# A transformer block on one core: two more tiles transposed by DMA, and work moved between slots and engines

## The chip, the core and the metric

The kernel runs on one core of a Trainium2 chip. A core has a matrix engine (TensorE, PE in the profile, with its weight loads as PEld), a vector engine (DVE), a scalar engine (ACT), GpSimd (POOL), and a sync engine (SP) that issues most DMAs here. Each engine works through its own queue in order and waits on semaphores where it needs what another has made. The metric is the device time of one execution in microseconds (us); 2% and less matter here, so times are compared as medians of several runs.

## What is computed

One pre-norm transformer block on x of 2048 positions by 512 channels, in float32: attention over a dilated local window, then a dense MLP with a squared ReLU.

```python
def _A_ref(x, wqkv, wo):           # H = 32 heads of 16, W = 8, dil = 2
    qkv = ...(x @ wqkv)...
    idx = pos[:, None] - (jnp.arange(W) * dil)[None, :]
    logits = jnp.einsum("bhsd,bhswd->bhsw", q, kg) * scale
    attn = _softmax(jnp.where(mask, logits, -1e9))
    o = jnp.einsum("bhsw,bhswd->bhsd", attn, vg)
    return o @ wo
def _B_ref(x, w1, b1, w2, b2):     # F = 1792
    r = relu(x @ w1 + b1)
    return (r * r) @ w2 + b2
h = x + _A_ref(_layernorm(x), wqkv, wo)
out = h + _B_ref(_layernorm(h), w1, b1, w2, b2)
```

## The kernel before

**Tiles and halves.** The positions are cut into 16 tiles of 128, four tiles to a group. Every operand of a matmul is split into a high half, a rounded copy made by ACT (`hi`, L151), and a low half, the difference, made by DVE or POOL (`lo`, L154, recorded as L155). A product is three sets of matmuls: high by high, low by high, high by low (`mm3`, L218; L228 in the profile). One product of a 128 x 512 tile is 12 matmuls.

**Phases.** First, 16 short products of the q, k, v projection; then a first phase (`first_phase`, L1007) that goes on with this projection for tiles 4 to 15, two tiles at a time, each as six half-products; then the MLP in four stages, u = 0 to 3, one for each group of four tiles. Stages 0 to 2 (L1087) have 17 steps p: at each step TensorE makes one block of w1's product (`mlp1`) and, three steps later, that block's product with w2 (`mlp2`, L895). Attention on DVE and POOL runs beside all this, as far as stage 2.

**Attention.** For each item (two rows of positions, two or four groups of heads), DVE multiplies q and k (L339), reduces (L373), and multiplies weights and v (L350); POOL adds up these products in three steps (`add_up`, L407), the last of which writes the result `o`. `stream` is a generator of these steps.

**The slots.** The order on all engines is written out by the program. `end_slot(pe)` (L122) closes a slot: it adds the planned TensorE time `pe`, runs what is registered for this slot with `at` (the list `due`), then `pump`s the attention generator until its planned DVE time has caught up with TensorE's, then runs what is registered with `midway` (the list `amid`; `pump` itself runs it once DVE's plan is within `HALF` = 2.6 us of TensorE's), then what is registered with `after` (the list `late`). So in DVE's queue a chore in `due` stands ahead of the slot's attention work, and a chore in `late` behind it. In the first phase a slot is half a product; `k` counts these halves from 0 to 23 over tiles 12 to 15, and `chores(k)` runs right after the slot before it is closed.

**From attention to the MLP, tile by tile.** At `OT[t]` the result of tile t is transposed on TensorE (`o_T`, L592): four 128 x 128 transposes into one PSUM bank, then `hi_T` and `lo_T`, both registered in `due`. At `WO[t]` follows its product with wo (`wo_product`, L683), and from it, slots later, the residual `h` and its norm's sums (`h_add`, L659, with `norm_stats`, L159), the normalised residual `hn` (`h_norm`), `add_b2` and a store of h (`spill`). The norm's three small factors are made on POOL by `finish` (L168). The normalised residual must then be transposed, too, to be the moving operand of stage u: by TensorE (`h_T`, L697), or, for tiles in `HV`, by DMA: ACT splits it into two 16-bit planes (`h_split`, L616), SP issues a transposing DMA (`turn_dma`, L618), ACT joins the planes (`turn_join`, L623), and `h_parts` (L648) makes the halves. In the first phase `HK[t]` gives the slots of the split and of the join, `HT[t]` that of `h_parts` or of `h_T`. Groups 1 to 3 are treated the same way inside stages 0 to 2, at the steps `OP`, `WP`, `HP`; all their attention results are transposed by DMA (`OV`).

**Banks of PSUM.** All eight are in use. Transposes of x and o in the first phase take turns in two, tr0 and tr1, one for each call (`Turn`, L139). A bank may be written again when the last reader of what it held is done. For x (`x_T`, L468) these are `hi_T`, registered in `due`, and `lo_T`, registered in `late`:

```python
def x_T(t):
    tr = transposes(xt.pop(t))
    xT[t] = row("xh", (P, KB, P), F32R), row("xl", (P, KB, P), F32R)
    at(0, hi_T, tr, [xT[t][0]])
    after(0, lo_T, tr, [xT[t][0]], [xT[t][1]])
```

Tiles 14 and 15 of x are transposed at k = 7 and 8 (`XT`). In `chores` this comes first, and then, in a loop over t, `o_T`, the split and join, `wo_product` and `h_parts` of tile t.

**Weights.** In the first phase `weight_job` (L570) loads a piece of wo or w1 and, five slots later, makes its halves. In stage 0 `split_w2` (L1069) makes the halves of w2's block f at step p = f: the high one on ACT, the low one on POOL in `late`.

Of the kernel before, what the change touches and what calls it, by code (L numbers as in the profile page):

```python
# [31 lines left out]
HALF = 2.6  # L32
AS = (8, 9, 12, 13)
OV = tuple(range(4, 16))
HV = (0,1,4,5,8,9,12,13)
SLOW = 1.01, 1.08, 1.05
DELAY = 3
WJ = 2
XT = (9, 11), (7, 8)
OT = 4, 5, 10, 12  # L40
WO = 7, 9, 13, 15
HT = 20, 20, 21, 23
HK = (12, 18), (14, 19)
W2 = (18,)
LH = 3, 4, 10, 11
OP = 6, 7, 12, 13
WP = 9, 10, 13, 14
HP = 15, 15, 16, 16
UP = 14, 14, 15, 15
HL = (14, 0), (14, 1), (15, 0), (15, 1)  # L50
# [8 lines left out]
def block_kernel(ctx, tc, x, wqkv, wo, w1, b1, w2, b2, out):  # L59
    nc = tc.nc  # L60
# [39 lines left out]
    w2_h, w2_l = {}, {}  # L100

    def row(name, shape=(P, D), dt=F32):
        return work.tile(list(shape), dt, name=name, tag="row", bufs=ROWS)
# [9 lines left out]
    def at(delta, fn, *a):  # L113
        due.setdefault(now["slot"] + delta, []).append((fn, a))

    def after(delta, fn, *a):
        late.setdefault(now["slot"] + delta, []).append((fn, a))

    def midway(delta, fn, *a):
        amid.setdefault(now["slot"] + delta, []).append((fn, a))  # L120
# [15 lines left out]
    def dve(t):  # L136
        now["dve"] += t
# [13 lines left out]
    def hi(dst, src):  # L151
        nc.scalar.copy(dst, src)  # L152
# [6 lines left out]
    def norm_stats(key, src):  # L159
        st = small.tile([P, 6], F32, name="st")  # L160
        mv = small.tile([P, 2], F32, name="mv", bufs=4)
        rs = small.tile([P, 2], F32, name="rs", bufs=4)
        nc.vector.bn_stats(st, src)
        nc.vector.bn_aggr(mv, st)
        dve(0.93)
        stats[key] = mv, rs

        def finish():  # L168
            nc.gpsimd.tensor_scalar(out=rs[:, 1:2], in0=mv[:, 1:2], scalar1=EPS, scalar2=None,
                                    op0=ALU.add)  # L170
            nc.gpsimd.tensor_tensor(out=rs[:, 0:1], in0=rs[:, 1:2], in1=mhalf, op=ALU.pow)  # L171
            nc.gpsimd.tensor_scalar(out=rs[:, 1:2], in0=mv[:, 0:1], scalar1=rs[:, 0:1],
                                    scalar2=-1.0, op0=ALU.mult, op1=ALU.mult)
        after(0, finish)

    def act_stats(key, src):

# [262 lines left out]
    def x_stats(t):  # L440
        if t < XS:
            norm_stats(t, xt[t])
        else:
            act_stats(t, xt[t])
# [125 lines left out]
    def weight_job():  # L570
        h, l, src, k, c0, cn = jobs.pop(0)
        raw = row("raw")
        nc.sync.dma_start(raw[:, :cn], src[k * P:(k + 1) * P, c0:c0 + cn])

        def split():
            hi(h[:, k, c0:c0 + cn], raw[:, :cn])
            after(0, lo, nc.gpsimd, l[:, k, c0:c0 + cn], raw[:, :cn], h[:, k, c0:c0 + cn])
        at(5, split)


    hs, hn = {}, {}
# [10 lines left out]
    def o_T(t):  # L592
        s, j = divmod(t, RI)
        pump(until=s)
        tr = transposes(o_t[s][:, j, :])
        if t % R == RI:

            ohl = att.tile([P, 2, KB, P], F32R, name="ohl", tag="o", bufs=3)
            oT[t] = ohl[:, 0], ohl[:, 1]
        else:  # L600
            oT[t] = row("oh", (P, KB, P), F32R), row("ol", (P, KB, P), F32R)
        at(0, hi_T, tr, [oT[t][0]])
        at(0, lo_T, tr, [oT[t][0]], [oT[t][1]])
# [55 lines left out]
    def h_add(t, ps):  # L659
        h = hs[t]  # L660
        nc.vector.tensor_tensor(out=h, in0=ps, in1=h, op=ALU.add)
        dve(0.7)
        if t in AS:
            after(0, act_stats, t, h)
        else:
            norm_stats(t, h)
# [16 lines left out]
    def wo_product(t, slots):  # L683
        ps = turn["mm"].tile("wo")
        oh, ol = oT.pop(t)
        mm3(ps, lambda k: oh[:, k, :], lambda k: ol[:, k, :],
            lambda k: wo_h[:, k, :], lambda k: wo_l[:, k, :], lows_last=t in OV)
        for n, (fn, a) in zip(slots, ((h_add, (t, ps)), (h_norm, (t,)), (add_b2, (t,)),
                                      (spill, (t,)))):
            (after if fn in (h_norm, spill) else at)(n + (fn is add_b2), fn, *a)  # L690
# [6 lines left out]
    def h_T(t):  # L697
        if t // R == R - 1:
            return last_h_T(t)
        tr = transposes(hn.pop(t), "mm")  # L700
        i = t % R
        hs_, ls_ = [a[:, :, i] for a in hh], [a[:, :, i] for a in hl]
        if len(turn["mm"].tags) > 2:
            at(0, hi_T, tr, hs_)
        else:
            due.setdefault(now["slot"], []).insert(0, (hi_T, (tr, hs_)))
        at(0, lo_T, tr, hs_, ls_)
# [299 lines left out]
    def first_phase(t0):  # L1007
        def chores(m):
# [11 lines left out]
            if jobs and m % 3 == 0:  # L1020
                at(0, weight_job)
# [3 lines left out]
            for t in range(R):  # L1025
                if k == OT[t]:
                    at(0, load_h, t)
                    o_T(t)
                if t in HV and k == HK[t][0]:
                    at(0, h_split, t)  # L1030
                    after(0, turn_dma, ("h", t))
                if t in HV and k == HK[t][1]:
                    at(0, turn_join, ("h", t))
                if k == WO[t]:
                    wo_product(t, (1, 3, 4, 6))
                    now["pe"] += 2.73
                if k == HT[t]:
                    (at(0, h_parts, t) if t in HV else h_T(t))
            if k in W2:
# [29 lines left out]
    def split_w2(f):  # L1069
        raw = raws.pop(f)  # L1070
        hi(w2_h[f], raw)
        if f < 12:
            place[f] = free.pop(0)
            w2_l[f] = big_l[:, place[f]]
            at(1, stash, f)
        after(0, lo, nc.gpsimd, w2_l[f], raw, w2_h[f])

    def stash(f):
        nc.sync.dma_start(w2l_d[f], w2_l[f].bitcast(F32))
# [7 lines left out]
    for u in range(R - 1):  # L1087
# [11 lines left out]
        for i in js:  # L1099
            t = R * (u + 1) + i  # L1100
            if not end:
                a = i // 2 if u == 2 else 0
                o0 = OP[i] - a - (2 if i >= RI and t in OV else 0)
                if t in OV:
                    turned = [(o0, at, 0, o_split, t), (o0, at if i >= RI else after, i // RI, turn_dma, ("o", t)),
                              (o0 + 2, at, 0, o_join, t)]
                else:
                    turned = [(o0, o_T, t)]
                if t in HV:
                    h0 = 11 + i  # L1110
                    turned += [(h0, midway, 0, h_split, t), (h0, after, 0, turn_dma, ("h", t)),
                               (h0 + 2, at, 0, turn_join, ("h", t))]
                for p, *what in ((LH[i] - a, at, 0, load_h, t), *turned,
                                 (WP[i] - a, wo_product, t, (0, 1, 2 + 3 * a, 3 + 3 * a))):
                    todo.setdefault(p, []).append(what)
                p, h = (HP[i], i % 2) if u < 2 else HL[i]
                if t in HV:
                    todo.setdefault(p, []).append((at, 0, h_parts, t))
# [14 lines left out]
        for p in range(FB + LAG):  # L1133
            more = 0.0
            if p == FB:
                run(due)
                dve(HOLD)
            if u < 2 and p == FB - 2:
                dve(HOLD)
            for fn, *a in sorted(todo.get(p, []), key=lambda x: x[0] is wo_product):  # L1140
                fn(*a)
                more += 2.73 if fn is wo_product else 0.0
            if p < FB:
                mlp1(u, fs[p])
                more += 2.73
                if first:
                    at(0, split_w2, p)
                    if p + 1 < FB:
                        load_w2(p + 1)
            q = p - LAG  # L1150
            if q >= 0:
                f = fs[q]
                mlp2(u, f, acc, js, q == 0, q == FB - 1,
                     (lambda: half(p)) if p in halves else None)
                more += 2.74
                if f < 12 and (need or first and p < FB - LAG):
                    free.append(place.pop(f))
                    if need:
                        at(1, fetch, need.pop(0))
            end_slot(more)  # L1160
# [85 lines left out]
```

## Time and profile before

| | |
|---|---|
| median of 3 runs | 510.37 us (509.52 to 511.27) |
| the profiled execution | 510.24 us |
| its span, first to last instruction | 508.5 us |
| granted TensorE clock | 1.000 |
| DMA | 102.61 MB, mean 202 GB/s |

The span leaves out 1.74 us at both ends of the execution. A matmul is pipelined: it lasts about 390 ns in the records, but the next one of 512 columns starts 227 ns after it, so waiting is read from the starts. A row of a timeline has the start and the length in us, the engine, the line, the operation, what is written from what, the count, and in brackets the idle time ahead of it with what ended it.

### The profile page before, as it was taken

Reading aid. Unit: us, or ns where it says so; the run is one execution under the profiler, and the core shown is the slowest. Engines: PE = TensorE matmul, PEld = TensorE weight load, DVE = VectorE, ACT = ScalarE, POOL = GpSimd, SP = SyncE. Lnnn points to the kernel's source line nnn. Section 1 sums busy time; section 2 is a strip of 40 time slices with the busy share of each in tenths; the row PEclk is TensorE's granted clock in tenths of the full one; section 3 lists DMA queues with packets and bytes.
Section 4 is the critical chain, followed back from the end, with each engine's and each line's share of the span. In section 5 each row is a group of like instructions: output and inputs, shape, how many; then the busy total and the mean of one; then the engine's idle time right before and its main releaser. Section 6 shows DMA issues by size and latency. Waiting matters only on the chain.

```text
span 508.5 us, 7542 instructions
## 1 busy us (share of the span) xinstructions
PE 498.6 (98%) x2422; PEld 420.5 (83%) x2422; DVE 375.2 (74%) x507; ACT 305.3 (60%) x558; POOL 361.4 (71%) x439
## 2 busy tenths in 40 slices
PE   8999999999999999999899999999999999999997
PEld 7998778888888887787688888888888888998986
DVE  6479899999999778986898989988951137732233
ACT  4635687577447747478454548756457847566541
POOL 5714789895776999989959777977896364685610
PEclk9999999999999999999999999999999999999999
DMA  8678889899698799789576756997572272444212
GB/s 271 189 212 204 245 290 302 245 307 303 201 228 253 253 273 278 215 216 291 166 248 207 216 147 165 257 252 244 161 173 63 80 212 83 169 123 144 64 43 83
DMA packets 109359, 102.61 MB, mean 202 GB/s; under 512 B 29448, under 2 KB 77832, under 8 KB 109320
## 3 DMA queue, kind: packets, MB, share of 16 engines
q1 hardware_dynamic: 108376, 101.61, 68.0%
q10 hardware_dynamic: 944, 0.52, 0.3%
q8 instruction: 19, 0.31, 0.2%
q14 instruction: 20, 0.16, 0.1%
HBM read 72.65 MB, written 24.25 MB: 191 GB/s over the span
## 4 chain that ended last, share of the span: by engine, by line
PE 66%; POOL 14%; DVE 2%; issue 2%; DMA 2%; ACT 1%; SPq 0%; POOLq 0%; ACTq 0%; DVEq 0%
PE mm L228 30%; PE acc L895 22%; PE wo L228 6%; PE mm L818 6%; POOL pr L407 5%; POOL rl L155 3%; POOL big_l L155 3%; PE tr L201 2%; POOL h L674 1%; DVE pr L350 1%; DMA q<-qkv_d 1%; DMA k<-qkv_d 1%; POOL o L407 1%; POOL w_x L155 1%; POOL rs L171 0%
## 5 line engine op out<-in xcount | busy, mean ns | idle before, releaser
L407 POOL TENSOR_TENSOR pr<-pr 128x512 f32<-128x512 f32 (+1 forms) x128 | 132.3, 1034 | 38.2 <-DVE pr L350 32.7
L228 PE MATMUL mm<-big_l,w_h 128*128 128x512 f32 x336 | 88.9, 391 | 0.7 <-ACT r L871 0.7
L350 DVE TENSOR_TENSOR pr<-ex,v 128x1024 f32<-128x1024 f32 x64 | 78.1, 1221 | 13.5 <-POOL o L407 10.1
L339 DVE TENSOR_TENSOR pr<-qp,k 128x1024 f32<-128x1024 f32 x64 | 76.8, 1200 | 9.3 <-ACT qp L268 8.4
L373 DVE TENSOR_REDUCE ex<-pr 128x64 f32<-128x1024 f32 x64 | 78.5, 1227 | 2.0
L228 PEld LDWEIGHTS mm<-big_l,w_h 128*128 128x128 f32 x336 | 62.8, 188 | 15.0 <-ACT r L871 2.0
L155 POOL TENSOR_TENSOR rl<-r,rh 128x512 fp32r<-128x512 f32 x42 | 55.6, 1326 | 14.9 <-ACT rh L152 14.9
L228 PE MATMUL mm<-big_l,xh 128*128 128x512 f32 (+1 forms) x208 | 55.8, 378 | 0.0
L228 PE MATMUL mm<-big_h,xh 128*128 128x512 f32 (+1 forms) x208 | 53.8, 379 | 1.3 <-ACT xh L152 1.3
L228 PE MATMUL mm<-big_h,xl 128*128 128x512 f32 (+1 forms) x208 | 52.7, 375 | 0.1
L895 PE MATMUL acc<-big_l,rh 128*128 128x512 f32 x190 | 52.2, 390 | 0.0
L895 PE MATMUL acc<-big_h,rh 128*128 128x512 f32 x190 | 52.1, 391 | 0.0
L895 PE MATMUL acc<-big_h,rl 128*128 128x512 f32 x190 | 51.7, 389 | 0.0
L871 ACT ACTIVATE r<-mm,b_sb 128x512 f32<-128x512 f32 x42 | 28.8, 685 | 33.6 <-PE mm L228 30.3
L228 PE MATMUL mm<-big_l,w_l 128*128 128x512 f32 x168 | 44.9, 389 | 0.0
L228 PEld LDWEIGHTS mm<-big_h,xh 128*128 128x128 f32 x208 | 37.6, 188 | 8.6 <-ACT xh L152 3.0
L228 PEld LDWEIGHTS mm<-big_h,xl 128*128 128x128 f32 x208 | 38.2, 188 | 6.4 <-DVE xl L155 0.5
L895 PEld LDWEIGHTS acc<-big_h,rl 128*128 128x128 f32 x190 | 35.7, 188 | 7.4
L895 PEld LDWEIGHTS acc<-big_l,rh 128*128 128x128 f32 x190 | 35.5, 188 | 7.4
L228 PEld LDWEIGHTS mm<-big_l,xh 128*128 128x128 f32 x208 | 37.5, 188 | 4.9
L895 PEld LDWEIGHTS acc<-big_h,rh 128*128 128x128 f32 x190 | 34.9, 188 | 6.7
L228 PEld LDWEIGHTS mm<-big_l,w_l 128*128 128x128 f32 x168 | 31.5, 188 | 6.6
(165 smaller groups left out, 917.8 us busy)
## 6 DMA issues: line engine op xcount, KB each, us to landing
k<-qkv_d SPq DMA_DIRECT2D x48, 288.0 KB, 3.1
v<-qkv_d SPq DMA_DIRECT2D x48, 288.0 KB, 3.6
qkv_d<-y SPq DMA_DIRECT2D x18, 512.0 KB, 5.1
big_l<-w2l_d SPq DMA_DIRECT2D x24, 256.0 KB, 3.1
xt<-in_A_x_dram SPq DMA_DIRECT2D x16, 256.0 KB, 4.7
q<-qkv_d SPq DMA_DIRECT2D x32, 128.0 KB, 3.7
h<-in_A_x_dram SPq DMA_DIRECT2D x16, 256.0 KB, 3.3
h_d<-h SPq DMA_DIRECT2D x16, 256.0 KB, 3.8
```

The lines of the kernel that those rows point to most:

```text
L155: eng.tensor_tensor(out=dst, in0=src, in1=h, op=ALU.subtract)
L201: nc.tensor.transpose(tr[:, k, :], src[:, k * P:(k + 1) * P], ident)
L228: nc.tensor.matmul(ps, l(k), r(k), start=(n == 0), stop=(n == 3 * KB - 1))
L339: nc.vector.tensor_tensor(out=pr.rearrange("p i w h d -> p i w (h d)"), in0=qps["now"][:, j % 2].unsqueeze(2).to_broadcast([P, RI, W, GC]) ...
L350: nc.vector.tensor_tensor(out=p2, in1=vwin, op=ALU.mult, in0=e1[:, :, :, j * GH:(j + 1) * GH].unsqueeze(4).to_broadcast([P, RI, W, GH, DH]))
L373: nc.vector.tensor_reduce(out=lf[:, :, :, j * GH:(j + 1) * GH], in_=pr, axis=X, op=ALU.add)
L407: nc.gpsimd.tensor_tensor(out=dst, in0=p2[:, :, :w], in1=p2[:, :, w:2 * w], op=ALU.add)
L674: nc.gpsimd.tensor_tensor(out=h, in0=h, in1=b2_sb, op=ALU.add)
L818: nc.tensor.matmul(ps, sta[y][:, k], mov[x][:, k], start=(first and q == 0), stop=(last and q == len(terms) - 1), skip_group_check=True)
L871: nc.scalar.activation(r, ps, AF.Relu, bias=b1_sb[:, f:f + 1])
L895: nc.tensor.matmul(acc[j], l[:, j * P:(j + 1) * P], w[f], start=(first and n < len(js)), stop=(last and n >= len(terms) - len(js)))
```

## The change

Two more tiles, 2 and 3, are in `HV`, with their slots in `HK`; `HT[2]` is 22 instead of 21, the slot of `h_parts`. Their attention results are transposed at k = 7 and 9 instead of 10 and 12, and their wo products come at 11 and 13 instead of 13 and 15. In stages 0 to 2 the first two tiles of the next group have their attention results at steps 5 and 6 instead of 6 and 7, and their wo products at 8 and 9 instead of 9 and 10. `finish` of `norm_stats` is registered in `amid` instead of `late`. The split of a weight piece is registered in `late` instead of `due`. Of w2's 14 blocks, the low halves of f = 1, 4, 7, 10 and 13 are made by DVE instead of POOL, at a planned 0.8 us each.

```diff
-HV = (0,1,4,5,8,9,12,13)
+HV = (0,1,2,3,4,5,8,9,12,13)
-OT = 4, 5, 10, 12
-WO = 7, 9, 13, 15
-HT = 20, 20, 21, 23
-HK = (12, 18), (14, 19)
+OT = 4, 5, 7, 9
+WO = 7, 9, 11, 13
+HT = 20, 20, 22, 23
+HK = (12, 18), (14, 19), (16, 20), (18, 22)
-OP = 6, 7, 12, 13
-WP = 9, 10, 13, 14
+OP = 5, 6, 12, 13
+WP = 8, 9, 13, 14
...
@@ norm_stats
-        after(0, finish)
+        midway(0, finish)
...
@@ weight_job
-        at(5, split)
+        after(5, split)
...
@@ split_w2
-        after(0, lo, nc.gpsimd, w2_l[f], raw, w2_h[f])
+        eng = nc.vector if f % 3 == 1 else nc.gpsimd
+        after(0, lo, eng, w2_l[f], raw, w2_h[f])
+        if eng is nc.vector:
+            dve(0.8)
```

## Prediction

> **What bounds the kernel now.** I read the page's busy line and its chain first, then the chain in order of time, the windows of the two middle stages and the TensorE timeline where the gaps are.
>
> ```profile
> span 508.5 us, 7542 instructions
> ...
> PE 498.6 (98%) x2422; PEld 420.5 (83%) x2422; DVE 375.2 (74%) x507; ACT 305.3 (60%) x558; POOL 361.4 (71%) x439
> ...
> PE 66%; POOL 14%; DVE 2%; issue 2%; DMA 2%; ACT 1%; SPq 0%; POOLq 0%; ACTq 0%; DVEq 0%
> ```
>
> TensorE is busy in 498.6 of 508.5 us, so a change can win only a few microseconds: the idle ones and the matmuls that it removes. Whatever makes TensorE wait anew is paid nearly in full. The 14% of POOL in the chain says where idle time can be won.
>
> ```profile
> 161.60 1.09 PE L228 MATMUL mm<-big_l,w_h 128*128 128x512 f32 x4
> ...
> 254.98 10.88 PE mm L228 x48
> ...
> 343.12 10.88 PE mm L228 x48
> ...
> 161.60:255.00 93.40, 90.17 (x394) 72.50 (x393) 78.47 (x98) 58.72 (x97) 85.70 (x92) 1.00 0.82 238
> 255.00:343.10 88.10, 88.10 (x393) 72.66 (x393) 79.15 (x95) 54.10 (x92) 68.67 (x80) 1.00 0.75 213
> ...
> 202.71 1.20 PE L228 MATMUL wo<-wo_h,oh 128*128 128x512 f32 x4
> 205.66 1.21 PE L228 MATMUL wo<-wo_h,ol 128*128 128x512 f32 x4 [0.84 <-DVE ol L155]
> 252.94 0.66 PE L201 MATMUL tr<-ident,hn 128*128 128x128 f32 x4 [1.45 <-ACT hn L196]
> ```
>
> The MLP's first stage (u = 0) starts at 161.60 and the second at 254.98: 93.38 us. The second, with the same matmuls, takes 343.12 - 254.98 = 88.14. So the first stage holds **5.2 us of TensorE waiting**, and it is the stage with the most POOL work (85.70 against 68.67 us; the columns are TensorE, its weight loads, DVE, ACT, POOL). Stages 1 and 2 have next to nothing to give.
>
> **The change part by part.**
>
> (1) *Eight transposes go.* A tile's four cost what stands between them and the next matmul, and a slow restart:
>
> ```profile
> 124.70 0.60 PE L201 MATMUL tr<-ident,xt 128*128 128x128 f32 x4
> 125.06 1.17 PE L228 MATMUL wo<-wo_h,oh 128*128 128x512 f32 x4
> 126.08 1.08 PE L228 MATMUL wo<-wo_h,ol 128*128 128x512 f32 x4
> ...
> 127.91 0.62 PE L228 MATMUL mm<-big_l,xh 128*128 128x512 f32 x2
> ...
> 129.28 0.60 PE L201 MATMUL tr<-ident,xt 128*128 128x128 f32 x4
> ```
>
> 125.06 - 124.70 = 0.36, and 1.17 - 1.08 = 0.09 for the restart: 0.45 a tile, **-0.9 us** for tiles 2 and 3.
>
> (2) *Attention results of tiles 2 and 3 transposed at k = 7 and 9 instead of 10 and 12.* Here I expect the change to lose. The tr banks alternate. Before, the order is o0, o1, x14, x15, o2, o3, so x14 and x15 have different banks. Afterwards it is o0, o1, x14, **o2**, x15, o3: x15 comes into the bank of x14, and may be written only when x14's low half has been taken from it. That subtraction stands in `late`, behind the slot's whole share of attention on DVE.
>
> ```profile
> 119.67 0.60 PE L201 MATMUL tr<-ident,o 128*128 128x128 f32 x4
> ...
> 120.35 0.59 ACT L152 CAST oh<-tr 128x512 fp32r<-128x512 f32 x1
> ...
> 121.03 0.69 DVE L155 TENSOR_TENSOR ol<-tr,oh 128x512 fp32r<-128x512 f32 x1 [0.58 <-ACT oh L152]
> ...
> 125.43 1.16 DVE L339 TENSOR_TENSOR pr<-qp,k 128x1024 f32<-128x1024 f32 x1
> ...
> 130.49 0.68 DVE L155 TENSOR_TENSOR xl<-tr,xh 128x512 fp32r<-128x512 f32 x1
> ```
>
> Slot k = 7 has 4.54 us of planned TensorE time (half a tile, x14's transposes, the first wo product), for which DVE gets the attention work from 125.43 to 130.49, 5.06 us, and only then x14's subtraction. The change puts o2's subtraction ahead of all that, and it waits: o2's transposes come behind wo product 0, at 127.91; by o0's rows ACT starts 120.35 - 119.67 = 0.68 later and DVE another 0.68, at 129.27. DVE idles from about 125.4 until then, is done with o2 at 129.9, with the slot's attention at 134.9, with x14 at 135.6. TensorE comes to x15 at 129.28 + 0.45 = 129.73. It stands for **+5.9 us**. In-order, everything behind waits too: the other wo products, and in DVE's queue the products that feed POOL. Bounds: were o2 ready at once, x14 would still end at 130.49 + 0.68 + 0.69 = 131.9, a stall of 2.1; nothing makes it longer than 5.9 but a late q load. The trace shows the order and durations from which 5.9 follows, so I take it. o3 at k = 9 needs o2's bank, free by then, but holds DVE once more behind wo product 1.
>
> (3) *Residuals 2 and 3 by DMA.* ACT gains two splits and two joins and SP two transposes; the joins are due only four slots after the splits, and the last high half one slot before stage u = 0, whose first matmul reads all four tiles.
>
> ```profile
> 152.69 0.59 ACT L523 COPY y<-mm 128x512 f32<-128x512 f32 x1
> 153.18 1.18 ACT L625 COPY pl<-hn 128x1024 uint16<-128x1024 uint16 x1
> ...
> 156.51 1.33 ACT L152 CAST big_l<-pl 128x256 fp32r<-128x256 f32 x4
> 157.74 0.64 ACT L152 CAST big_l<-tr 128x256 fp32r<-128x256 f32 x2
> 158.60 0.59 ACT L523 COPY y<-mm 128x512 f32<-128x512 f32 x1 [0.22 <-PE mm L228]
> ...
> L616 ACT COPY pl<-hn x8: 1041/1042/1049, 139.1 to 406.7; 128x1024 uint16<-128x1024 uint16 x8
> ...
> DMA to landing us min/median/max: 6.0/6.7/7.0
> ...
> h<-in_A_x_dram SPq DMA_DIRECT2D x16, 256.0 KB, 3.3
> ```
>
> On the clock of before: slot k = 18 begins on ACT with y at 152.69 and the join of tile 0 at 153.18, which ends 154.3; tile 3's split (1.04) then ends at 155.3 and its DMA starts. With the landing of the residual's transposes, 6.7, it is there at 162.0; the join (1.18) ends at 163.2, the first half of the cast (1.33 / 4 = 0.33) at 163.5. TensorE would want it at 161.60 - 0.9 = 160.7: **+2.8 us**. Bounds: the landings shown are only those that ACT waited for; at 3.3, as a load of a tile has, ACT reaches the join after the copy of 158.60 and tile 2's cast (0.64) at 159.8, is done at 161.3 with half a cast: 0.6. At 7.0 it is 3.1. I take the residual's own row, since the queue is as full here. Nothing else hides it: there is no other matmul to do before the stage, and behind the waiting join stand ACT's cast of tile 3 and its copy of the last y. SP issues the two transposes behind the splits; the k and v loads queued behind them wait for DVE to free their buffers anyway.
>
> [...]
>
> (4) *Five of fourteen low halves of w2 from POOL to DVE, and the norm's factors sooner on POOL.*
>
> ```profile
> L155 POOL TENSOR_TENSOR big_l<-raw,big_h 128x512 fp32r<-128x512 f32 x12 | 15.6, 1298 | 0.0
> ...
> L155 DVE TENSOR_TENSOR ol<-pl,oh 128x512 fp32r<-128x512 f32 x9 | 7.5, 830 | 1.5 <-ACT oh L152 1.5
> ...
> L155 DVE TENSOR_TENSOR ol<-tr,oh 128x512 fp32r<-128x512 f32 x3 | 2.1, 692 | 2.4 <-ACT oh L152 2.3
> ...
> 163.56 2.12 POOL L407 TENSOR_TENSOR pr<-pr 128x512 f32<-128x512 f32 x2 [4.29 <-DVE pr L350]
> ```
>
> POOL loses 5 x 1.30 = 6.5 us of its 85.70; DVE gains 5 x 0.83 = 4.2, and is busy 78.47 of 93.40, so has 14.9 idle. The stage's excess of 5.2 lies in wo's halves (late because DVE's products waited for POOL) and in the last residual at 252.94, whose factors came late from POOL. 6.5 is more than 5.2, but two of the five (f = 10 and 13) come in its last slots, and the relief comes piecemeal. Bounds: 0, and -5.2; I take **-4.0**, three quarters, nearer the full excess because POOL's list has hardly a gap in this stage.
>
> DVE's subtraction takes 830 ns with both inputs in SBUF and 692 with one in PSUM. [...] If each of the five blocked POOL for its 0.83, the relief would be 6.5 - 4.2 = 2.3 instead of 6.5, and the term about -1.5; this is rival D's way.
>
> Does (2) cost the same when POOL is on the chain from 157 on? POOL was itself idle for 4.29 us before 163.56, waiting for DVE, and DVE is held for 3.8 us by o2 and again by o3, so POOL starts the stage as late as TensorE does.
>
> (5) *Weight casts to the end of their slot.* In the first phase ACT stood for a weight load ahead of a transposed tile:
>
> ```profile
> 60.12 0.62 ACT L152 CAST wo_h<-raw 128x512 fp32r<-128x512 f32 x1 [2.35 <-DMA raw<-in_A_wo_dram]
> 60.65 0.58 ACT L523 COPY y<-mm 128x512 f32<-128x512 f32 x1
> 61.12 0.59 ACT L152 CAST xh<-tr 128x512 fp32r<-128x512 f32 x1
> 61.76 1.20 PE L228 MATMUL mm<-big_h,xh 128*128 128x512 f32 x4 [0.60 <-ACT xh L152]
> ```
>
> The copy of y goes ahead of the cast, so xh comes 0.47 sooner at most, but DVE's half is late as well: 0 to -0.6, **-0.3**.
>
> (6) *Later groups a slot sooner* (stages 0 to 2). Both stages behind the first have no excess to win, and these products only change places: 0. If the results were not there, ACT would wait ahead of TensorE's next bank; I see no cause, and take 0 with 0.5 either way.
>
> Sum: -0.9 + 5.9 + 2.8 - 4.0 - 0.3 = **+3.5 us**. The profiled execution took 510.24 us (span 508.5 and 1.74 around it), 0.13 under the median of 510.37. Forecast: **513.7 us**.
>
> **The rivals.**
>
> A, the forecast: both stalls, most of the first stage's excess won. With (3) from 0.6 to 3.1 and (4) from -5 to -2.5 it reaches from 510.5 to 515.5. Chance 0.62.
>
> B, no change: the 5.9 stays, but the first stage's whole excess goes, since POOL keeps its lead while TensorE stands, and tile 3's transposes land early: -0.9 + 5.9 + 0.6 - 5.2 - 0.3 = +0.1, 510.3. For it: POOL is what the chain runs on from 157, and 5.9 us more for it would be all it lacks; against: DVE feeds POOL and is held itself. Chance 0.14.
>
> C, faster: x15 finds its bank free. This decides: x14's subtraction would have to end on DVE before 129.7. Then (2) costs nothing, and the sum is -0.9 + 2.8 - 4.0 - 0.3 = -2.4, 507.8, and down to 504.5 with the whole 5.2 and an early landing. For it: only that I may have an order wrong; against: xl at 130.49 is already too late in the kernel before. Chance 0.12.
>
> D, slower still: the five subtractions lock POOL and wait on DVE, so that (4) gives 0 to 1.5: +7.5 to +6.0, 516.2 to 517.7. For it: 830 against 692 ns. Against: 14.9 us of idle DVE. Chance 0.12.
>
> **The numbers.** A measurement of this kernel tells about 0.3% from no change: 508.8 to 511.9. Slower by more: D and nearly all of A, 0.12 + 0.57 = 0.69. Within: A's lower end and most of B, 0.05 + 0.12 = 0.17. Faster: C and the rest of B, 0.14. The range from 509.5 to 517.0 holds A, B and half of D, about 0.82; C and the end of D are left out.
>
> **What would show it.** The stall of (2): a gap of some 6 us before x15's transposes, released by DVE's xl, and a DVE gap of 3.8 us before o2's ol. The stall of (3): a gap before the first mm of u = 0, released by ACT's cast of tile 3, with ACT waiting for the hn transposes. (4): stage 0 takes about 89 us from its first mm to that of stage 1. If x15 starts without a wait, the forecast is wrong by its largest term.

## The result and the profile after

| | before | after |
|---|---|---|
| median | 509.94 us (508.67 to 511.27) | **532.06 us** (531.57 to 532.63) |
| ratio, 95% interval | | **1.0434** (1.0403 to 1.0465) |
| the profiled execution, its span | 510.24, 508.5 us | 531.57, 529.8 us |
| granted TensorE clock, mean | 1.000 | 0.984 |

The change costs 22 us. The forecast was 513.7 with a range to 517.0: the sign was right, the size far off. The busy line and the chain of the page after:

```profile
span 529.8 us, 7523 instructions
...
PE 504.1 (95%) x2414; PEld 423.9 (80%) x2414; DVE 376.7 (71%) x512; ACT 308.7 (58%) x562; POOL 356.0 (67%) x434
...
PE 28%; POOL 4%; DVE 2%; issue 1%; ACT 1%; DMA 1%; POOLq 0%; ACTq 0%; DVEq 0%
```

TensorE executes eight matmuls fewer, yet is busy 504.1 us instead of 498.6: some of its matmuls last longer, which a wait can't do. The chain's shares add to only 37%, since it is followed back to 332.81 us only; it says nothing of the stalls ahead of that. So the span is cut at the first matmul of each stage. The columns are the lengths of the stretches between the first wo product, the first matmuls of stages u = 0 to 3, and the end of the last matmul:

| | first wo to u = 0 | stage 0 | stage 1 | stage 2 | stage 3 |
|---|---|---|---|---|---|
| before | 36.53 | 93.22 | 88.14 | 87.98 | 74.15 |
| after | 49.49 | 94.70 | 90.41 | 92.58 | 74.16 |
| difference | +12.96 | +1.48 | +2.27 | +4.60 | +0.01 |

More than half is lost ahead of stage 0, where the prediction had +7.8 (-0.9 + 5.9 + 2.8). Stage 0 should have won 4.0, and stages 1 and 2 should have stayed. What TensorE waited for, over the span (us in total, times, longest), is the shortest view of the causes:

```profile
PE mm L228 <- ACT y L523: 6.3, 1, 6.3
PE tr L201 <- DVE xl L155: 5.8, 1, 5.8
PE tr L725 <- ACT hn L196: 2.8, 1, 2.8
PE wo L228 <- ACT ohl L152: 2.6, 2, 1.8
```

None of the four is in the same view of before, whose longest wait is 1.4 us. The TensorE and DVE timelines of after, at the second of them:

```profile
128.90 1.09 PE L228 MATMUL mm<-big_h,xl 128*128 128x512 f32 x4
135.80 1.09 PE L201 MATMUL tr<-ident,xt 128*128 128x128 f32 x4 [5.81 <-DVE xl L155]
136.54 2.06 PE L228 MATMUL mm<-big_h,xh 128*128 128x512 f32 x4
```

```profile
125.22 0.34 DVE L379 RECIPROCAL sm<-sm 128x32 f32<-128x32 f32 x1
129.25 0.69 DVE L155 TENSOR_TENSOR ohl<-tr,ohl 128x512 fp32r<-128x512 f32 x1 [3.69 <-ACT ohl L152]
...
133.84 1.22 DVE L339 TENSOR_TENSOR pr<-qp,k 128x1024 f32<-128x1024 f32 x1
134.98 0.68 DVE L155 TENSOR_TENSOR xl<-tr,xh 128x512 fp32r<-128x512 f32 x1
```

This is step (2) as predicted, almost to the digit: o2's subtraction at 129.25 (forecast 129.27) after a DVE gap of 3.69 (3.8), x14's at 134.98 (134.9), and x15's transposes behind it. The transposes themselves and the matmuls behind the gap are what was not predicted: four transposes take 1.09 us instead of 0.60, four matmuls 2.06 instead of 1.07. The windows of after, a wait and the matmuls behind it, three times (columns as before, then the granted clock, the DMA share and GB/s):

```profile
129.70:135.80 6.10, 0.29 (x2) 0.03 (x1) 6.03 (x8) 0.89 (x2) 2.45 (x3) 0.69 0.35 99
135.80:139.20 3.40, 3.40 (x11) 2.87 (x12) 2.02 (x4) 1.05 (x2) 1.73 (x4) 0.55 0.96 270
168.20:174.60 6.40, 0.12 (x1) 0.00 (x0) 3.05 (x7) 5.37 (x13) 0.00 (x0) 0.88 0.93 215
174.60:179.90 5.30, 5.26 (x13) 4.15 (x14) 4.91 (x7) 0.50 (x1) 3.15 (x4) 0.51 0.78 231
443.40:446.20 2.80, 0.00 (x0) 0.00 (x1) 2.69 (x4) 2.77 (x6) 1.73 (x2) 0.98 0.13 32
446.20:449.60 3.40, 3.40 (x11) 2.88 (x11) 2.35 (x4) 1.76 (x5) 1.78 (x1) 0.52 0.79 260
```

After each of the three waits TensorE works for 3.4 to 5.3 us at about **half the clock**. Matmul starts lie 427 ns apart there, 227 elsewhere, so each such stretch holds TensorE up by an estimated 1.5 to 2.6 us on top of its wait: half of the 3.08, 5.21 and 3.29 us for which it works at a clock of 0.50 (last section). Whether the span pays that depends on what the stage waits for otherwise: after the first wait it does (experiment 4), at the start of stage 0 it doesn't (experiment 6).

The ACT timeline of after, ahead of stage 0:

```profile
162.75 0.82 ACT L196 ACTIVATE hn<-h,rs 128x512 f32<-128x512 f32 x1 [3.15 <-POOL w_l L155]
...
165.01 1.04 ACT L616 COPY pl<-hn 128x1024 uint16<-128x1024 uint16 x1
...
172.03 1.16 ACT L625 COPY pl<-hn 128x1024 uint16<-128x1024 uint16 x1 [1.03 <-DMA hn<-pl]
173.09 0.37 ACT L268 COPY qp<-q 128x256 f32<-128x256 f32 x1
173.40 0.70 ACT L152 CAST big_l<-pl 128x256 fp32r<-128x256 f32 x2
174.01 0.57 ACT L523 COPY y<-mm 128x512 f32<-128x512 f32 x1
```

TensorE goes on at 174.63, with the end of that last copy of y. Its timeline:

```profile
174.63 2.08 PE L228 MATMUL mm<-big_l,w_h 128*128 128x512 f32 x4 [6.31 <-ACT y L523]
```

This is step (3) with another size: 6.31 us, not 2.8.

### The profile page after: what moved, and what is told of

Its sections match the earlier page's. It is cut to its first block, busy times and chain, and to the rows that moved or that the text cites. A ratio compares the mean times of both kernels' runs of the same rounds, so it can differ in the third digit from the quotient of the medians.

```text
span 529.8 us, 7523 instructions
## 1 busy us (share of the span) xinstructions
PE 504.1 (95%) x2414; PEld 423.9 (80%) x2414; DVE 376.7 (71%) x512; ACT 308.7 (58%) x562; POOL 356.0 (67%) x434
## 5 line engine op out<-in xcount | busy, mean ns | idle before, releaser
L228 PE MATMUL mm<-big_l,w_h 128*128 128x512 f32 x336 | 90.3, 396 | 6.9 <-ACT y L523 6.3
L350 DVE TENSOR_TENSOR pr<-ex,v 128x1024 f32<-128x1024 f32 x64 | 78.1, 1222 | 13.5 <-POOL o L407 10.9
L228 PEld LDWEIGHTS mm<-big_l,w_h 128*128 128x128 f32 x336 | 64.1, 191 | 21.3 <-ACT y L523 6.7
```

Source lines behind the costliest of these rows:

```text
L228: nc.tensor.matmul(ps, l(k), r(k), start=(n == 0), stop=(n == 3 * KB - 1))
L350: nc.vector.tensor_tensor(out=p2, in1=vwin, op=ALU.mult, in0=e1[:, :, :, j * GH:(j + 1) * GH].unsqueeze(4).to_broadcast([P, RI, W, GH, DH]))
```

## The experiments

Each kernel differs from one of the two by a few lines. "First wo to u = 0" and the stages are the columns of the table above.

**1. Is the first wait the bank, and what do the moved parts cost without it?** Both start from the kernel after. In the first, x14's low half goes ahead of the slot's attention; in the second, tiles 2 and 3 are treated as before.

```diff
# e1_xl_first, on after
-        after(0, lo_T, tr, [xT[t][0]], [xT[t][1]])
+        (at if t == 14 else after)(0, lo_T, tr, [xT[t][0]], [xT[t][1]])
# e2_tiles_back, on after
+HV = (0,1,4,5,8,9,12,13)
+OT = 4, 5, 10, 12
+WO = 7, 9, 13, 15
+HT = 20, 20, 21, 23
+HK = (12, 18), (14, 19)
```

> The changed kernel with one thing moved: x14's low half is registered in due instead of late, so it is taken ahead of o2's and of the slot's attention work, and x15's bank is free when TensorE comes to it. Theory 1 (the bank wait is the first cause; it costs its 6.0 us and, behind it, some 1.5 us of matmuls at a lower granted clock, and DVE's idle time puts attention behind, which is paid again in stages 0 to 2): the wait before x15 is gone, and the time falls from 532 by at least 7 us, to 525 or lower, nearer 520 if part of the later waits goes with it. Theory 2 (the later waits come from the groups' results asked for a slot sooner, or from the low halves on DVE, and have nothing to do with the bank): 524 to 525, with stages 1 and 2 as long as in the changed kernel (90.4 and 92.6 us).

Measured: 525.4 us, ratio 1.0281 (1.0244 to 1.0318). The wait before x15's transposes and the slow matmuls behind it are gone, and first wo to u = 0 falls from 49.49 to 42.93 us. What is left there, 6.4 us over before, is the second wait (7.2 us, released by the copy of y).

> The changed kernel with tiles 2 and 3 treated as before: residuals transposed by TensorE, attention results at k = 10 and 12, wo products at 13 and 15. All else of the change stays: groups a slot sooner, w2's low halves on DVE, factors sooner, weight casts later. Theory 1: both long waits and the lag are gone, stage 0 keeps what the prediction gave it, 505 to 507 us. Theory 2: stages 1 and 2 keep their 2.3 and 4.6 us of waiting, 511 to 514 us.

Measured: 520.01 us, ratio 1.0185 (1.0151 to 1.022); first wo to u = 0 is 36.53, as before, and stages 0 to 2 take 94.30, 90.55 and 94.57. So parts (4) to (6), which the prediction had at -4.3, lose 9.4 us in this combination, more than either theory expected.

**2. The groups and the low halves.**

```diff
# e3_groups_back, on after
+OP = 6, 7, 12, 13
+WP = 9, 10, 13, 14
# e4_w2_dve, on before
-        after(0, lo, nc.gpsimd, w2_l[f], raw, w2_h[f])
+        eng = nc.vector if f % 3 == 1 else nc.gpsimd
+        after(0, lo, eng, w2_l[f], raw, w2_h[f])
+        if eng is nc.vector:
+            dve(0.8)
# e7_w2_uncharged, on before: the same without the last two lines
```

> The changed kernel with only the later groups back at their steps (attention results at 6 and 7, wo products at 9 and 10). Theory 1: little changes, 530 to 533, stages 0 to 2 still late by the lag. Theory 2: the waits of stages 0 to 2 (some 4, 2.3 and 4.6 us) go, 521 to 524.

Measured: 532.16 us, ratio 1.0413 (1.0372 to 1.0454), as after: the groups cost nothing there (theory 1).

> The kernel before with only the five low halves of w2 moved from POOL to DVE. The prediction's term for stage 0: its 93.2 us fall by 3 to 5 us, the time to 505 to 507. Theory 2, and the prediction's rival D: DVE and POOL hold each other up, stage 0 keeps its length, 510 or more.

Measured: 510.66 us, ratio 1.0001 (0.9983 to 1.0018). As the prediction had it, stage 0 falls to 90.46, and stage 1 rises to 91.33: **the 2.8 us won in one stage are lost in the next**, by waits that the kernel before does not have, the longest for DVE's low halves of the residual and for ACT's halves of attention results:

```profile
PE mm L228 <- DVE big_l L155: 0.9, 1, 0.9
PE wo L228 <- ACT ohl L152: 0.7, 1, 0.7
```

> The kernel before with five low halves of w2 on DVE, but without the planned 0.8 us each, so that attention keeps its place in the order. Theory P: stage 0 stays 2 to 3 us shorter, as it was with the charge (90.5 against 93.2 us), and stage 1 keeps the 88.1 us of before instead of 91.3: 507 to 508.5 in all. If stage 1 loses 3 us nevertheless, the charge is not the reason, and the DVE time itself, or DVE and POOL blocking each other, is.

Measured: 510.84 us, ratio 1.0011 (0.9999 to 1.0024); stage 0 takes 93.71 and stage 1 88.18, both as before, which neither reading of the expectation had. The subtractions are on DVE in both kernels; only the plan differs. So it was not the relief of POOL that shortened stage 0 in the kernel with the charge. The planned 4 us put attention off: DVE executes 102 instructions in stage 0 here and 98 with the charge. POOL is relieved here, too, 81.19 us busy in stage 0 instead of 85.70, but its waits for DVE's products (L350) grow from 5.6 to 9.0 us. Step (4)'s reason was wrong.

**3. The factors, and the groups alone.**

```diff
# e5_factors, on before
-        after(0, finish)
+        midway(0, finish)
# e6_groups_only, on before
+OP = 5, 6, 12, 13
+WP = 8, 9, 13, 14
```

> The kernel before with only the norm's factors registered in amid instead of late. Theory F (POOL, made to stand for DVE's sums ahead of attention's additions, holds attention up, and this is what tiles 2 and 3 do not explain): slower than 510.5 by 2 us or more, with stages 1 and 2 longer. Theory P (the plan has no DVE time to spare: the 4 us of it that the low halves are charged put attention off, and results asked for sooner then wait): the factors are harmless, 508.5 to 510.5, stage 0 shorter by about the 1.6 us that its last residual waited.

Measured: 512.47 us, ratio 1.0052 (1.0036 to 1.0069). Stage 0 takes 89.81, 3.4 us less than before, and stage 2 takes 92.83, 4.85 more. POOL's timeline in stage 2, of before and of this run:

```profile
414.56 0.73 POOL L786 TENSOR_TENSOR traw<-traw 128x256 f32<-128x256 f32 x1
...
417.00 0.74 POOL L789 TENSOR_TENSOR traw<-traw 128x256 f32<-128x256 f32 x1
418.38 0.35 POOL L169 TENSOR_SCALAR rs<-mv 128x1 f32<-128x1 f32 x1 [0.64 <-DVE mv L164]
```

```profile
415.52 0.34 POOL L169 TENSOR_SCALAR rs<-mv 128x1 f32<-128x1 f32 x1 [3.79 <-DVE mv L164]
...
417.26 0.73 POOL L786 TENSOR_TENSOR traw<-traw 128x256 f32<-128x256 f32 x1
...
419.69 0.74 POOL L789 TENSOR_TENSOR traw<-traw 128x256 f32<-128x256 f32 x1
```

Before, four sums (L786 to L789, of blocks of w1 for the last stage) stand ahead of the last tile's factors on POOL and fill the time until DVE has the statistics. With the factors moved forward, POOL stands 3.79 us for the statistics, and the sums come behind. ACT's cast of these sums waits in turn, and behind it, in ACT's queue, stands the last tile's residual. The ACT and TensorE timelines of this run:

```profile
420.46 1.05 ACT L152 CAST th<-traw 128x1024 fp32r<-128x1024 f32 x1 [7.75 <-POOL traw L789]
...
425.74 0.81 ACT L196 ACTIVATE hn<-h,rs 128x512 f32<-128x512 f32 x1
```

```profile
426.60 0.66 PE L725 MATMUL tr<-ident,hn 128*128 128x128 f32 x4 [2.90 <-ACT hn L196]
...
427.56 1.71 PE L895 MATMUL acc<-big_h,rl 128*128 128x512 f32 x4
```

The wait of 2.9 us is followed by slow matmuls (1.71 us for four instead of 1.07). The kernel after has the same wait, 2.8 us for L725.

> The kernel before with only the later groups' attention results and wo products a step sooner. Theory F: no change, 510 to 511. Theory P: alone it does little as well, since attention is on time in the kernel before: 510 to 513, and if it is slower, then through waits on DVE in stages 1 and 2.

Measured: 509.2 us, ratio 0.9977 (0.9965 to 0.999): 1.2 us faster, all of it in stage 0 (92.02); both theories expected no gain.

**4. The two waits ahead of stage 0.** The sooner wo products alone, with the residuals by DMA, and with TensorE kept at work during the wait:

```diff
# e8_wo_sooner, on before
+OT = 4, 5, 7, 9
+WO = 7, 9, 11, 13
# e9_turns_added: e8_wo_sooner with
+HV = (0,1,2,3,4,5,8,9,12,13)
+HT = 20, 20, 22, 23
+HK = (12, 18), (14, 19), (16, 20), (18, 22)
# e10_fill_wait: e8_wo_sooner with, ahead of x15's transposes
+                if early and m == 8:
+                    b = turn['tr'].tags[turn['tr'].n % 2]
+                    fill = psum.tile([P, D], F32, name='fill', tag=b).rearrange(...)
+                    for n in range(50):
+                        nc.tensor.transpose(fill[:, n % KB, :], ident, ident)
```

> The kernel before with only the attention results of tiles 2 and 3 at k = 7 and 9 and their wo products at 11 and 13; residuals still transposed by TensorE. The wait for x14's bank costs 6.0 us and some 1.6 us of slow matmuls after it, no long wait stands before stage 0, and what attention lost costs more later: 518 to 523. Without the lag: 518.

Measured: 519.36 us, ratio 1.0176 (1.0145 to 1.0207). First wo to u = 0 takes 44.56, 8.03 more than before: 5.98 of wait, some 1.5 of slow matmuls behind it (below), and 0.5 of other, small waits.

> The kernel before with the second and third part of the change alone: attention results of tiles 2 and 3 transposed sooner, their residuals transposed by DMA. The run with the sooner transposes alone took 44.56 us from the first wo product to the stage u = 0, where the kernel before took 36.53; the changed kernel took 49.49. If the residuals by DMA are the rest of that (theory R: tile 3's factors come late on POOL because DVE was held, so its DMA starts some 3 us later than the prediction had it, and behind the join stands the copy of y with its bank), this run takes 49 to 50 us there and 523 to 526 us in all. If they cost what the prediction gave them, 2.8 us less 0.9 for the transposes that go (theory S: the rest came from the low halves, the factors or the groups), it takes 46.5 there and 520.5 to 522 in all.

Measured: 525.15 us, ratio 1.0282 (1.0259 to 1.0305), and 50.75 us there: 6.2 more for the residuals by DMA. Theory R's size holds, with neither low halves, factors nor groups in the kernel; 50.75 is a little over what it expected. Its reason, that DVE was held, does not stand up to experiment 6.

> The sooner transposes alone, with 50 transposes of the identity added on TensorE ahead of the fifteenth tile-half's wait, into the bank that is free; nobody reads them. They fill some 6 us in which TensorE would stand. In the run without them the matmuls behind the wait start 427 ns apart instead of 227 for about 3.4 us, at a granted clock of 0.55. If it is the idle time ahead that lowers the clock (theory I), they start 227 ns apart here, and the run is 1.3 to 1.8 us faster than the one without, 517.5 to 518.2 us, with 42.8 to 43.3 us from the first wo product to u = 0. If the clock drops for another reason, such as the load of DVE and POOL at that place (theory L), it takes 519.4 us and 44.6 us there, or more by what the added transposes overrun the wait.

Measured: 517.89 us, ratio 1.0138 (1.0113 to 1.0163), 43.10 us there. The windows of the sooner products alone, and of this run:

```profile
130.10:136.15 6.05, 0.24 (x3) 0.03 (x1) 5.98 (x8) 1.35 (x3) 2.89 (x4) 0.70 0.35 98
136.15:139.55 3.40, 3.40 (x11) 2.87 (x12) 2.02 (x4) 0.59 (x1) 1.70 (x4) 0.54 0.93 260
```

```profile
129.93:135.74 5.81, 5.68 (x51) 5.48 (x51) 5.74 (x7) 1.35 (x3) 2.90 (x4) 1.00 0.38 102
135.74:139.14 3.40, 3.40 (x17) 2.89 (x18) 1.96 (x4) 0.59 (x1) 1.72 (x4) 1.00 0.94 258
```

Same wait, same work of DVE, ACT, POOL and the DMA engines; with TensorE at work, the clock stays at 1.00 and 17 matmuls fit in the 3.4 us that held 11. **Here it is TensorE's own idle time that halves its clock** (0.54 with it, 1.00 without), and 1.5 us (44.56 - 43.10) were won by useless work.

**5. What is left of the change.** The factors sooner only below tile 12, with the groups; the weight casts alone:

```diff
# e11_best, on before
+OP = 5, 6, 12, 13
+WP = 8, 9, 13, 14
-        after(0, finish)
+        (midway if key < 12 else after)(0, finish)
# e12_casts, on before
-        at(5, split)
+        after(5, split)
```

> The kernel before with the groups a slot sooner and the factors ahead of the slot's end for the tiles below 12 alone, so that in stage u = 2 the sums of the attention still stand ahead of tile 15's factors on POOL. Theory F (the loss of stage u = 2 in the run with all factors sooner, 4.85 us, was this order on POOL, and the gain of stage u = 0, 3.4 us, is separate from it): stage u = 2 takes 88.0 us again, stage u = 0 some 89 to 90, and the time is 505.5 to 507.5 us. Theory G (the gain of stage u = 0 is attention put off, and comes back in a later stage wherever POOL is full): stage u = 0 is as short, stage u = 1 or u = 2 is longer by 2 us or more, and the time is 509 to 511 us.

Measured: **508.08 us, ratio 0.9953** (0.9937 to 0.9968), the best kernel here. Stage 0 takes 90.81, stages 1 and 2 88.10 and 87.98: the loss of stage 2 was that order on POOL, and the gain of stage 0 need not come back. (The sums in question are those of w1's blocks, L786 to L789, and not attention's, as the expectation calls them.) The two gains of stage 0, 3.4 and 1.2, do not add up: together they are 2.4, and the time is a little over what theory F expected.

> The kernel before with the fifth part of the change alone, the weight casts at the end of their slot. The prediction gave it -0.3 us, 0 to -0.6. If ACT's copy of y ahead of the cast frees the first phase as argued, 509.8 to 510.5 us; if the casts come late for the products that read the weights, 511 us or more, with waits for wo_h, w_h or their low halves on TensorE or POOL that the kernel before does not have.

Measured: 510.42 us, ratio 1.0005 (0.9988 to 1.0022): nothing.

**6. Whose is the second wait?** Both start from the best kernel; the sooner wo products come without their first wait, and then tile 2's residual by DMA as well.

```diff
# e13_wo_mended: e11_best with
+OT = 4, 5, 7, 9
+WO = 7, 9, 11, 13
-        after(0, lo_T, tr, [xT[t][0]], [xT[t][1]])
+        (at if t == 14 else after)(0, lo_T, tr, [xT[t][0]], [xT[t][1]])
# e14_tile2_dma: e13_wo_mended with
+HV = (0,1,2,4,5,8,9,12,13)
+HT = 20, 20, 22, 23
+HK = (12, 18), (14, 19), (16, 20), (18, 22)
```

> The kernel before with the groups sooner and the factors sooner below tile 12, as in the best run so far (508.08 us; 36.54 us from the first wo product to u = 0, stage u = 0 90.8), and with the attention results of tiles 2 and 3 transposed sooner, tile 14's low half made ahead of the slot's attention on DVE. Their residuals stay on TensorE. If the bank was the whole of the loss of the sooner products (theory M), 36.5 to 37.5 us there and 507 to 509.5 in all. If the products in themselves hold DVE and with it the attention (theory H), a stall of the bank is gone but 1 us or more is lost there or in stage u = 0: 509.5 to 512.

Measured: 510.59 us, ratio 1.0002 (0.9988 to 1.0015); first wo to u = 0 takes 38.71, 2.2 more than in the best kernel. No wait stands before x15 any more, but the first matmul of u = 0 waits 1.7 us for DVE's low half of a residual. The sooner products bring nothing even without their stall, as theory H had it. They do not even make tile 3's normalised residual sooner: ACT makes it 31.0 us after the first wo product, behind a wait for POOL, and 29.2 us after it both in the best kernel and in the kernel before.

```profile
156.00 0.82 ACT L196 ACTIVATE hn<-h,rs 128x512 f32<-128x512 f32 x1 [2.98 <-POOL rs L172]
```

> The same with tile 2's residual by DMA as well; tile 3's stays on TensorE. If the second wait is tile 3's alone, by its late factors and its landing (theory T), the first matmul of u = 0 waits for nothing new: 0.45 us less than the run without it, 36.1 to 37 us from the first wo product to u = 0, 506.5 to 509 us in all. If it is the ACT work of each tile, 1.04 for a split, 1.16 for a join and 0.7 for half a cast, that stands ahead of the last copy of y (theory Q), tile 2's half of the earlier 6.4 us is seen here: 39 to 40 us there and 510 to 512 us in all.

Measured: 513.14 us, ratio 1.0039 (1.0025 to 1.0053), and 40.80 us there. With 42.93 for both tiles (the first run, which has the other parts of the change too), the steps are 36.5, 38.7, 40.8, 42.9: 2.2 for the sooner products, and **about 2.1 us for each tile's residual**. Theory Q's size is nearly met, both figures a little above it; tile 3's landing is not the point. ACT's timeline of this run, where tile 3 is transposed by TensorE:

```profile
156.77 0.82 ACT L196 ACTIVATE hn<-h,rs 128x512 f32<-128x512 f32 x1 [3.18 <-POOL w_l L155]
157.49 0.56 ACT L523 COPY y<-mm 128x512 f32<-128x512 f32 x1
157.96 2.23 ACT L625 COPY pl<-hn 128x1024 uint16<-128x1024 uint16 x2
...
161.80 1.17 ACT L625 COPY pl<-hn 128x1024 uint16<-128x1024 uint16 x1
162.86 0.58 ACT L523 COPY y<-mm 128x512 f32<-128x512 f32 x1
...
164.25 0.65 ACT L152 CAST big_l<-tr 128x256 fp32r<-128x256 f32 x2
164.78 0.61 ACT L523 COPY y<-mm 128x512 f32<-128x512 f32 x1
```

From 156.77 on ACT has no gap: it waited 3.18 us for POOL, and then everything the stage needs stands in its queue, 8.6 us of it, up to the last copy of y; TensorE starts at 165.44. No row waits for a DMA, and none does in the first kernel of experiment 1, where tile 3 goes by DMA as well.

The ACT work that theory Q names is only half of tile 2's 2.1 us. Its split stands ahead of the wait for POOL, in time in which ACT is idle; its join (1.17) stands behind it. The other half is that the wait itself ends later: with POOL's subtraction of a weight piece (w_l, 155.58 to 156.74), though tile 3's factors were done at 155.61. In the run without tile 2's DMA it ended with the factors. So tile 3's normalised residual comes another 1.1 us later. By the program `hn` and the weight pieces take their buffers from the same pool of rows, which would explain the wait; no run tested it. For tile 3 in the first kernel of experiment 1 both its split and its join stand behind that wait, 2.2 us. And the wait for POOL is not DVE's doing, as theory R had it: without the stall it is as long (3.15 us in that kernel, 2.98 and 3.18 in these two).

The two kernels of this experiment also show a half clock that the span doesn't pay. Stage 0 begins at full clock in the first and at half clock in the second, yet takes 91.77 and 91.76 us. Its first 5.89 us, without tile 2's DMA and with it:

```profile
163.73:169.62 5.89, 5.89 (x26) 4.89 (x27) 5.46 (x7) 2.24 (x4) 2.88 (x4) 1.00 0.64 159
```

```profile
165.44:171.33 5.89, 5.89 (x14) 4.68 (x15) 5.50 (x7) 0.83 (x2) 3.62 (x4) 0.50 0.72 190
```

## Why the prediction was wrong, step by step

(1) **Eight transposes less, -0.9.** The eight matmuls are gone. But the four transposes of a tile also took a turn in the banks of the products. Without them the last copy of y, which before ran at 161.79 beside the first matmul of u = 0 (161.60), releases that matmul in the kernel after (174.01 + 0.57, then 174.63). By ACT's last row this costs the 0.6 us of the copy. In the run with the sooner products alone, which keeps the eight, the same matmul starts at 170.05, beside the copy at 170.03. That the turn of the banks is the reason is read from the program; no run changed it alone.

(2) **x15's transposes wait, +5.9.** The mechanism and the wait were right (+5.97, shown by the run that removed it and the one that made it alone). What failed is the price: a wait was charged at its length. Behind it TensorE ran at 0.55 of its clock, and with the small waits the term was 8.0, not 5.9. The prediction asked how long TensorE would stand, and not how it would run when it went on. Behind the second long wait it is the same, at 0.51.

(3) **The residuals by DMA, +2.8.** The place was right and the size wrong: 4.9 between the run with the sooner products and the kernel after, 6.2 between that run and the one with the residuals added. In the kernel after, the last matmul ahead of the stage starts at 167.94 and the stage's first 6.69 us later, 6.47 more than usual. Three things lie between 2.8 and that. The chain had tile 3's split 6.4 us ahead of the time at which TensorE is due (154.3 and 160.7), which would be 161.8 here; it began at 165.01, **3.2 us late**, since ACT stood 3.15 us for POOL (by the profile for the subtraction w_l, which ended at 162.72; tile 3's factors were done at 161.59). The DMA, issued at 166.08, landed 5.9 later and not 6.7 (-0.8). And behind the join stood the copy of q, the second half of the cast and the copy of y, 1.1 us. 2.8 + 3.2 - 0.8 + 1.1 = 6.3. The step that failed took ACT's rows of before for granted, as if the engines that feed ACT kept their lead over TensorE: the chain was followed back to ACT's queue, but not to POOL's. And it charged one tile; the runs show that tile 2, whose landing was in time, costs as much, half of it by its join on ACT and half by a longer wait of ACT for POOL.

(4) **Low halves and factors, -4.0.** Both parts do shorten stage 0, alone, by 2.8 and 3.4. Two steps failed. The low halves gain by the plan's 0.8 us each, which puts attention off, and stage 1 gives it back; moved without the charge they gain nothing, though POOL was 4.5 us less busy there (of the 6.5 forecast). (The excess to win was 5.1 and not 5.2: 254.98 is where a piece of the chain begins, and the stage's last matmul gives way to stage 1's first at 254.82.) And the factors were moved past the sums of stage 2 in POOL's queue: "what is late next" was asked for stage 0 alone, though `finish` runs 14 times (L169) and as late as stage 2. That cost 4.85 in its own run, and 4.6 in stage 2 of the kernel after.

(5) **Weight casts, -0.3.** 0: within what the step allowed.

(6) **Groups sooner, 0 with 0.5 either way.** Alone -1.2, in stage 0, which did have excess to win; inside the whole change 0.

The sum: 8.0 + 4.9 ahead of stage 0 (forecast 7.8 with the transposes), +1.5 in stage 0 (-4.0), +2.3 in stage 1 (0) and +4.6 in stage 2 (0): 21.3, against a difference of the spans of 529.8 - 508.5 = 21.3. Rival C, that x15 finds its bank free, fell at once. D was right that the low halves win next to nothing. Its mechanism is there, but small. The 830 ns that spoke for it are the mean of 673 to 1301, with a median of 702. In the kernel before, a subtraction on POOL that starts beside one on DVE (232.94 and 232.92) lasts 1.81 us instead of 1.30; in the kernel after, a moved one on DVE that starts during one on POOL (182.65 and 182.17) lasts 1.36 us instead of 0.68. In the run with the subtractions uncharged the five last 0.68 to 1.60 us on DVE. That fits a relief of POOL by 4.5 us and not 6.5. But even the 4.5 did not shorten the stage, so this did not decide it.

What stays open: alone, (4) to (6) sum to +1.9 us by their ratios (0.1 for the low halves, 2.7 for the factors, 0.3 for the casts, -1.2 for the groups, of 510 us), together they lose 9.4. The waits in stage 2 are traced; why the gains of stage 0 vanish when they are combined isn't. In the kernel after, the longest wait inside stage 0 is for ACT's halves of attention results (1.8 us; 0.8 more in stage 1), so attention is late, but which part makes it so was not separated.

## What to carry to other kernels

A stall of TensorE cost its length and then, behind every wait of 2.21 us or more whose clock is shown here, matmuls at half clock (0.50 to 0.55). Where nothing else bounds what follows, price it with 1.5 to 2.6 us on top, the estimate from the kernel after. When a piece of code that serves many tiles is moved in a queue, look at the rows around each of its uses, the last one above all, and not only at the stage that it is meant to help. And an item of a plan that shortens one stage must be followed to the next: a part that only puts work off shows no gain in the end.

## What was not expected of the hardware

The prediction charged a wait at its length and had no slower clock behind it. After the 2.85 us wait that ends at 446.20 of the kernel after the clock was 0.52 for 3.4 us, and after one of 2.21 us in the run with tiles 2 and 3 as before it was 0.55. After 1.72 us, in the mended run ahead of stage 0, it was 1.00, and so it was after the 1.82 us that the kernel after waits at 246.16 for ACT's halves. The windows of the second and the third of these:

```profile
234.30:236.80 2.50, 0.40 (x2) 0.00 (x0) 2.47 (x4) 0.64 (x1) 2.34 (x4) 0.93 1.15 283
236.80:240.20 3.40, 3.30 (x8) 2.65 (x9) 2.75 (x4) 3.34 (x5) 3.40 (x4) 0.55 1.05 324
```

```profile
161.61:163.73 2.12, 0.40 (x3) 0.03 (x1) 2.12 (x6) 2.12 (x7) 0.61 (x2) 1.00 1.07 360
163.73:167.10 3.37, 3.37 (x15) 2.80 (x16) 3.33 (x5) 0.65 (x2) 0.51 (x1) 1.00 0.51 142
```

In the trace of the kernel after the clock is either 1.00 or 0.50, and changes at these times (two stretches at half clock and the one between them):

```profile
132.05:138.88 6.83, 3.08 (x10) 2.62 (x11) 5.74 (x8) 1.05 (x2) 3.85 (x7) 0.50 0.75 208
138.88:173.01 34.13, 29.44 (x132) 24.03 (x130) 22.20 (x33) 18.50 (x30) 21.06 (x28) 1.00 0.78 194
173.01:179.84 6.83, 5.21 (x12) 4.14 (x13) 5.96 (x7) 2.09 (x6) 3.09 (x4) 0.50 0.67 201
```

The third half clock lasts from 446.08 to 449.49. So the stretches are 6.83, 34.13, 6.83, 266.24 and 3.41 us long: 2, 10, 2, 78 and 1 times 3.413. TensorE pays for what is left of a slow stretch when its wait is over: 3.08, 5.21 and 3.29 us. The first fall came 2.06 us after TensorE's last matmul had ended, the second 4.69 us after. What sets these lengths no run shows, and how long TensorE must be idle for the clock to fall stays open: 1.82 us lowered nothing and 2.21 us were enough, and no wait shown here lies between them.
